# Attention output stored once in fp32 and split where it is used, and a tenth unit of seven products in the first expert block

## The chip, the cores and the metric

The kernel runs on one core of a Trainium2 chip. A core has a matrix engine (TensorE, PE in the profile), three engines that work on tiles (VectorE, DVE; ScalarE, ACT; GpSimd, POOL) and a sync engine (SyncE, SP) that here only issues DMAs. The metric is the device time of one execution in microseconds; lower is better.

## The reference

An attention with a memory gate writes x, and a gated expert layer works on x:

```python
scores = scale * np.matmul(q, k.transpose(0, 1, 3, 2))     # q, k, v: 4 x 8 heads x 576 x 64
scores = np.where(causal, -1000000000.0, scores)
a = np.exp(scores - scores.max(-1, keepdims=True))
a /= a.sum(-1, keepdims=True) + 1e-09
local = np.matmul(a, v)
mem_out = (phi(q) @ M_prev) / (phi(q) . z_prev + 1e-06)    # phi(x) = elu(x) + 1
x = g * mem_out + (1 - g) * local                          # 2304 tokens x 512
gate, val = x @ w_gate, x @ w_val                          # 512 x 1536 each
out = (silu(gate) * val) @ w_out                           # 1536 x 512
```

All inputs and the output are fp32.

## The kernel before

**Attention.** The 32 heads are 16 pairs. The loop runs over n = 0 to 16; iteration n makes the scores of pair n and the values of pair n-1. The score tiles are `s` in PSUM, `ps`, `pl` and `p` (short, long and last key ranges) in SBUF. The DVE reads scores with a mask and a running maximum, ScalarE takes the exponential, the DVE makes the inverse sums `rs`, and POOL scales `ps`, `pl` and `p` by them; PE transposes the scaled tiles (`tr`, copied to `g`) and multiplies with the values. POOL also splits q and k of the pair after, `qh`, `kh` by a rounding copy and `ql`, `kl` by a subtract, so that a product of fp32 numbers is made of three matmuls, high x high, high x low and low x high. `ph` is phi(q) on the DVE.

**Leaving.** At the end of a pair `leave` takes its 576 columns of x out of PSUM in two parts (256 and 320): ScalarE copies the high part into `xh`, the DVE subtracts it from the PSUM tile into `xl`. Both go to DRAM, into `xdh` and `xdl`.

**Weights.** 12 slices of `w_gate`, `w_val` and `w_out` come as pairs of words (`wraw`); a slice is made of thirds, each taken through a clamp, a move and a word (`third_clamp`, `third_move`, `third_word`: `wa`, `we` and `wr`), split into high and low (`wgh`, `wgl`, `woh`, `wol`) and, made ready, stored to `wdr` and `wdo`. Some thirds are made in the attention loop, one step at the end of an iteration (`EARLY`), most in the first block of the experts.

**Experts.** 36 units, three blocks of 768 tokens (`ORDER`) by 12 slices of 128 of d_ff. Of a block, x stands as four pieces in halves of tokens (i) and of channels (j): `p1` (0,0), `p2` (0,1), `p7` (1,0), `p4` (1,1), each as a high and a low tile. The first `PLAIN` units of the first block use `eight`: four groups of 12 matmuls of 384 columns. All others use `seven`: seven products of 6 matmuls on seven mixtures of the pieces, `p1`, `p2`, `p6`, `p7`, `p5`, `p4`, `p3` in this order, with weight mixtures (`operands`) that the DVE and ScalarE make in the unit before. `p6`, `p5`, `p3` and the second `p7` are mixtures of the pieces (`sums` makes them in `xr`, `xt`, `xm`; `spreads` splits them into high and low). Each unit ends in `weigh`, which multiplies silu of the gate half (`zg`, `zh`) by the value half and splits the result into `uh` (ScalarE) and `ul` (DVE, in `halves`, a step later). The groups of the second matrix, `lower`, three matmuls of 512 columns, run one unit later, a group between two steps.

PE's steps write in turns to two PSUM banks (`ring`), so a step starts when the engines have emptied the bank of the step but one before it.

**What sets the order.** Every engine but SP runs in the order of the code (`queued`, which adds a dependence to every instruction; nearly all instructions therefore stand at its line, L84, in the profile). SP's order is set by a scheduler. In a unit, `plan[k]` lists the work that stands behind step k, and `arrive` what goes into the next unit's plan.

## Time and profile before

| | |
|---|---|
| runs | 612.06 us median of 3 (612.0 to 612.1) |
| profiled execution | 611.38 us, of which the span is 609.6 |
| granted TensorE clock | 0.996 of full speed |
| PE busy | 599.6 us (98%) |
| DVE busy | 485.0 us (80%) |
| ACT busy | 395.2 us (65%) |
| POOL busy | 214.8 us (35%) |
| attention loop | to 187.7 us |
| expert units | from 187.8 us |

The span is the time in which the engines of the profiled execution worked. The median is of other executions; times inside the kernel are from the profiled one. Busy shares are averages over two stages that use the engines differently: POOL, for one, works in the attention loop and in the first expert block, and not after it.

### The profile page before, as it was taken

How to read it: one execution, taken by the hardware profiler on the slowest of the kernel's cores; microseconds unless marked ns; L12 is line 12 of the kernel's file. 1: busy time of each engine (PE TensorE's matmuls, PEld its weight loads, DVE VectorE, ACT ScalarE, POOL GpSimd, SP SyncE). 2: the span in 40 equal slices, each digit the busy share in tenths (PEclk: the TensorE clock that was granted, in tenths of full speed). 3: DMA queues.
4: the chain of work that ended last, by engine and by line, in shares of the span. 5: the costliest groups of instructions: out<-in, count | busy, mean ns of one | idle time of the engine just before them, and what ended most of it. 6: DMA issues, size and time to landing. Idle time of an engine off the chain costs nothing.

```text
span 609.6 us, 11282 instructions
## 1 busy us (share of the span) xinstructions
PE 599.6 (98%) x3794; PEld 531.5 (87%) x3794; DVE 485.0 (80%) x1208; ACT 395.2 (65%) x917; POOL 214.8 (35%) x261
## 2 busy tenths in 40 slices
PE   6999999999999999999999999999999999999997
PEld 4878878778788999999899999999999999999996
DVE  6899999999988998898998665665888765665653
ACT  8788888888876777777656654454456654454442
POOL 7999999999963334334320000000000000000000
PEclk9999999999999999999999999999999999999999
DMA  8456756657337657799556622323755622332212
GB/s 250 133 159 178 255 171 204 215 179 216 141 117 277 187 182 239 239 361 282 192 175 208 217 92 70 112 96 115 232 184 177 211 100 69 107 103 69 70 35 103
DMA packets 49321, 102.46 MB, mean 168 GB/s; under 512 B 7024, under 2 KB 17136, under 8 KB 49264
## 3 DMA queue, kind: packets, MB, share of 16 engines
q1 hardware_dynamic: 48832, 101.32, 51.1%
q8 instruction: 30, 0.49, 0.3%
q10 hardware_dynamic: 432, 0.43, 0.2%
q14 instruction: 27, 0.22, 0.1%
HBM read 74.99 MB, written 26.74 MB: 167 GB/s over the span
## 4 chain that ended last, share of the span: by engine, by line
PE 96%; POOL 1%; DMA 1%; issue 0%; DVE 0%; ACT 0%; SPq 0%; ACTq 0%; DVEq 0%
PE s L84 60%; PE tr L84 36%; DMA qr<-in_qt_dram 1%; POOL ps L84 0%; POOL kl L84 0%; SPq L269 0%; ACT g L84 0%; POOL qh L84 0%; DVE rs L84 0%; ACT wa L84 0%; POOL pl L84 0%; DVE mem L84 0%; DVE pl L84 0%; SPq L560 0%; DVE pt L84 0%
## 5 line engine op out<-in xcount | busy, mean ns | idle before, releaser
L84 ACT ACTIVATE zh<-zh 128x384 f32<-128x384 f32 x33 | 17.4, 527 | 74.8 <-DVE zh L84 74.8
L84 POOL TENSOR_SCALAR pl<-pl,rs,og 128x384 f32<-128x384 f32 (+1 forms) x64 | 55.9, 886 | 9.4 <-DVE rs L84 9.4
L84 DVE TENSOR_TENSOR zv<-s,zv 128x384 f32<-128x384 f32 x33 | 18.4, 557 | 51.1 <-PE s L84 45.9
L84 PE MATMUL tr<-woh,ul 128*128 128x512 f32 x144 | 57.3, 398 | 0.0
L84 PE MATMUL tr<-woh,uh 128*128 128x512 f32 x144 | 57.0, 396 | 0.0
L84 PE MATMUL tr<-wol,uh 128*128 128x512 f32 x144 | 56.8, 394 | 0.0
L84 POOL TENSOR_SCALAR we<-we 128x512 f32<-128x512 f32 x32 | 24.9, 780 | 76.8 <-ACT we L84 76.7
L84 ACT ACTIVATE pl<-pl,mx 128x384 f32<-128x384 f32 (+1 forms) x64 | 42.3, 664 | 12.3 <-DVE mx L84 12.3
L84 PE MATMUL tr<-g,vp 128*64 128x320 f32 (+4 forms) x448 | 48.8, 360 | 0.3 <-ACT g L84 0.3
L84 DVE TENSOR_TENSOR tl<-tt,th 128x512 fp32r<-128x512 f32 x66 | 47.7, 723 | 0.0
L84 ACT CAST th<-tt 128x512 fp32r<-128x512 f32 x66 | 41.1, 622 | 9.6 <-DVE tt L84 6.3
L84 PEld LDWEIGHTS tr<-g,vp 128*64 128x64 f32 x448 | 29.4, 137 | 18.0 <-issue 2.3
L84 PE MATMUL s<-kh,qh 64*128 64x128 f32 (+4 forms) x160 | 37.2, 386 | 4.5 <-ACT kh L84 4.0
L84 ACT CAST uh<-zh 128x384 fp32r<-128x384 f32 x36 | 18.5, 513 | 32.6 <-DVE zh L84 32.3
L84 DVE TENSOR_TENSOR zg<-s,zp 128x384 f32<-128x384 f32 x33 | 18.4, 558 | 25.8 <-ACT bh L84 23.5
L84 DVE CUSTOM_DVE_ANT_0 pl<-s,maskp 128x384 f32<-128x384 f32 (+1 forms) x64 | 38.1, 615 | 0.3 <-PE s L84 0.3
L84 DVE TENSOR_TENSOR bl<-wr,bh 128x512 fp32r<-128x512 f32 x66 | 36.3, 550 | 0.0
L84 ACT CAST bh<-wr 128x512 fp32r<-128x512 f32 x66 | 33.9, 513 | 0.0
L84 PEld LDWEIGHTS tr<-woh,ul 128*128 128x128 f32 x144 | 27.1, 188 | 6.8 <-DVE ul L84 0.3
L84 ACT ACTIVATE ps<-ps,mx 128x128 f32<-128x128 f32 (+1 forms) x64 | 28.6, 453 | 6.4 <-DVE mx L84 6.4
L84 POOL TENSOR_SCALAR ps<-ps,rs,og 128x128 f32<-128x128 f32 (+1 forms) x64 | 32.0, 513 | 1.6 <-DVE rs L84 1.2
L84 DVE COPY g<-tr 128x384 f32<-128x384 f32 (+2 forms) x60 | 30.0, 518 | 2.7 <-PE tr L84 1.4
(198 smaller groups left out, 2000.4 us busy)
## 6 DMA issues: line engine op xcount, KB each, us to landing
wr<-wdr SPq DMA_DIRECT2D x24, 512.0 KB, 3.3
wraw<-in_wg_dram SPq DMA_DIRECT2D x12, 512.0 KB, 4.6
wraw<-in_wv_dram SPq DMA_DIRECT2D x12, 512.0 KB, 5.1
wraw<-in_wo_dram SPq DMA_DIRECT2D x12, 512.0 KB, 5.1
wol<-wdo SPq DMA_DIRECT2D x24, 256.0 KB, 2.8
woh<-wdo SPq DMA_DIRECT2D x24, 256.0 KB, 3.1
qr<-in_qt_dram SPq DMA_DIRECT2D x15, 384.0 KB, 3.2
vp<-in_v_dram SPq DMA_DIRECT2D x16, 320.0 KB, 4.1
```

What stands on the lines that cost most here:

```text
L84: ins = getattr(eng, name)(*args, **kw)
```

## The change

x is stored once, as fp32 (`xo` to `xd`), and split into high and low where it is used.

- `leave`: ScalarE copies both parts from PSUM into `xo`; the DVE has no part in it. One store in place of two.
- The first block's four pieces are loaded into their low tiles at the end of iterations 6, 8, 10 and 12. Behind it ScalarE rounds a half (384 columns) of a piece into its high tile per iteration (7 to 14), and an iteration later (8 to 15) the DVE subtracts it in place.
- `PLAIN` is 2: unit 2 is a seven-product unit, and its operands are made a unit earlier, in unit 1.
- `sums` loads the four pieces from `xd` (`begin`) and doesn't add anything; in the first block too, where the sums were taken from the high and low tiles in SBUF. The mixtures `xt`, `xm` and those written into `xr` are as before.
- At a block's end `p1`, `p2` and `p4` are split on chip too, as `p7` was; before, their high and low tiles were loaded.
- In `seven`, of the two `weigh` operations behind the last product, the one that reads its bank goes first, except in the last unit.
- `lower` runs in the order 0 to 5 in all units; before, in 3, 4, 5, 0, 1, 2 from unit 4 on.

```diff
@@ -29,7 +29,7 @@
-PLAIN = 3
+PLAIN = 2
@@ -52,8 +52,7 @@
     dram = ctx.enter_context(tc.tile_pool(name="dram", bufs=1, space=DRAM))
-    xdh = dram.tile([128, NPAIR, NT], F32, name="xdh")
-    xdl = dram.tile([128, NPAIR, NT], F32, name="xdl")
+    xd = dram.tile([128, NPAIR, NT], F32, name="xd")
@@ -165,9 +164,14 @@
 
     xs = {p: [near.tile([128, 2, N2], F32R, name=f"x{p}{part}") for part in "hl"] for p in ("p1", "p2", "p7", "p4")}
 
+    where = dict(p1=(0, 0), p2=(0, 1), p7=(1, 0), p4=(1, 1))
+
+    def x_block(t0, i, j):
+        return xd[:, 2 * j : 2 * j + 2, t0 + i * N2 : t0 + i * N2 + N2]
+
     thirds = [(0, 0), (0, 1), (0, 2), (1, 0), (1, 1)]
-    work_of = [[(3, 0), (3, 1)]]
+    work_of = [[(2, 0), (2, 1)]]
     work_of += [[(n, 2)] + [(n + 1 + (n >= PLAIN - 1), j) for j in range(2)] for n in range(1, NF - 2)]
@@ -505,11 +509,6 @@
-            def give(self, t0, src):
-                c = slice(t0 * 128, t0 * 128 + src.shape[1])
-                act.copy(self.xh[:, c], src)
-                return lambda: dve.tensor_tensor(self.xl[:, c], src, self.xh[:, c].bitcast(F32), op=ALU.subtract)
-
             def turns(self):
                 self.g1 = rot(sb, "g1", [128, 2, 384], F32, 1)
                 self.g2 = rot(sb, "g2", [128, 4, 2, 320], F32, 1)
@@ -540,19 +539,14 @@
 
             def leave(self):
                 first, rest = self.av
-                self.xh = rot(sb, "xh", [128, 576], F32R, NX)
-                self.xl = rot(sb, "xl", [128, 576], F32R, NX)
-                self.give(0, first[:, 0:256])()
+                x = rot(sb, "xo", [128, 576], F32, NX)
+                act.copy(x[:, 0:256], first[:, 0:256])
 
                 def ending():
-                    low = self.give(2, rest[:, 0:320])
-                    return lambda: (low(), self.d2())
+                    act.copy(x[:, 256:576], rest[:, 0:320])
+                    SP.dma_start(xd[:, self.pr, self.b * S : self.b * S + S], x)
 
                 return ending
-
-            def d2(self):
-                for dst, src in ((xdh, self.xh), (xdl, self.xl)):
-                    SP.dma_start(dst[:, self.pr, self.b * S : self.b * S + S], src.bitcast(F32))
...
@@ -576,13 +570,12 @@
                 cur.begin()
             if old:
                 old.turns()
-            low = ending()
+            ending()
             while copies:
                 copies.pop(0)()
             reads = [scores(t) for t in range(2)]
             reads[0](0)
             reads[0](1)
-            low()
             if n == 0:
                 cur.lows()
             reads[1](0)
@@ -680,10 +673,19 @@
                     third_word(act, dve, i, copies)
                 if n == at + 4 and i < 3:
                     low_part(dve)
+            for p, at in zip(("p1", "p2", "p7", "p4"), (6, 8, 10, 12)):
+                high, low = xs[p]
+                if n == at:
+                    SP.dma_start(low.bitcast(F32), x_block(ORDER[0], *where[p]))
+                for k in range(2):
+                    if n == at + 1 + k:
+                        act.copy(high[:, k], low[:, k].bitcast(F32))
+                    if n == at + 2 + k:
+                        dve.tensor_tensor(low[:, k], low[:, k].bitcast(F32), high[:, k].bitcast(F32), op=ALU.subtract)
             if n in AHEAD:
                 raw_load(AHEAD.index(n), loads.get(n + 2))
 
-        ending()()
+        ending()
         low_part(dve)
         i = len(EARLY) + 1
         third_clamp(pool, i)
@@ -739,42 +741,22 @@
         for p in ("p6", "p5", "p3"):
             xs[p] = [mbp.tile([128, 2, N2], F32R, name=f"x{p}{part}") for part in "hl"]
 
-        def block(x, t0, i, j):
-            return x[:, 2 * j : 2 * j + 2, t0 + i * N2 : t0 + i * N2 + N2]
-
-        def direct(t0, p, i, j):
-            for dst, src in zip(xs[p], (xdh, xdl)):
-                SP.dma_start(dst.bitcast(F32), block(src, t0, i, j))
-
-        def sums(t0, here=False):
+        def sums(t0):
 
             got = rot(mbp, "xr", [128, 4, 2, N2], F32, 1)
-            at = ((1, 0), (1, 1), (0, 0), (0, 1))
             a21, a22, a11, a12 = (got[:, n] for n in range(4))
             s1, s = (rot(mbp, name, [128, 2, N2], F32, 1) for name in ("xt", "xm"))
-            tmp = (s, s1)
-            mix = dict(p6=s, p7=a11, p5=s1, p3=a12)
-
-            def load(n):
-                for dst, src in ((got[:, n], xdh), (tmp[n % 2], xdl)):
-                    ld = SP.dma_start(dst, block(src, t0, *at[n]))
-                    follow(ld, last[DVE], "the loads that come before go first", mybir.DependencyClass.Sync)
-
-            def add(n):
-                if here:
-                    h, l = (x.bitcast(F32) for x in xs[("p7", "p4", "p1", "p2")[n]])
-                    dve.tensor_tensor(got[:, n], h, l, op=ALU.add)
-                    return
-                dve.tensor_tensor(got[:, n], got[:, n], tmp[n % 2], op=ALU.add)
-                if n + 2 < 4:
-                    load(n + 2)
+            mix = dict(p1=a11, p2=a12, p6=s, p7=a11, p5=s1, p4=a22, p3=a12)
+
+            def begin():
+                for n, at in enumerate(((1, 0), (1, 1), (0, 0), (0, 1))):
+                    SP.dma_start(got[:, n], x_block(t0, *at))
 
             tt = lambda out, a, b, op: (lambda: dve.tensor_tensor(out, a, b, op=op))
-            work = [lambda n=n: add(n) for n in range(4)] + [
-                tt(s1, a21, a22, ALU.add), tt(s, s1, a11, ALU.subtract), tt(a12, a12, s, ALU.subtract),
-                tt(a11, a11, a21, ALU.subtract),
-            ]
-            return lambda: (load(0), load(1)), work, mix
+            return begin, [
+                tt(s1, a21, a22, ALU.add), tt(s, s1, a11, ALU.subtract),
+                tt(a11, a11, a21, ALU.subtract), tt(a12, a12, s, ALU.subtract),
+            ], mix
 
         def high(mix, p, k):
             return lambda: act.copy(xs[p][0][:, k], mix[p][:, k])
@@ -907,14 +889,13 @@
             dve.tensor_tensor(g2, step(5, "p4", False), g2, op=ALU.add)
             act.activation(g2, g2, AF.Silu, scale=W_ONE)
             rest(5)
-            weigh(u, 1, g2, v2)
-            weigh(u, 0, g1, step(6, "p3", False))
+            ps = step(6, "p3", False)
+            for i, g, v in ((1, g2, v2), (0, g1, ps)) if final else ((0, g1, ps), (1, g2, v2)):
+                weigh(u, i, g, v)
             rest(6)
             return u
 
         first = units[0][0]
-        for p, i, j in (("p1", 0, 0), ("p2", 0, 1), ("p7", 1, 0), ("p4", 1, 1)):
-            direct(first, p, i, j)
         before = None
         spreads = lambda mix, *what: [
             (high if kind == "h" else low)(mix, p, k) for kind, p in what for k in range(2)
@@ -946,56 +927,44 @@
             arrive = []
             if plain:
                 if f == 0:
-                    _, due, mix = sums(t0, True)
-                    for k, some_ in enumerate(((0,), (1,), (2, 4), (3,))):
-                        plan[k] += [due[i] for i in some_]
+                    begin, due, mix = sums(t0)
+                    begin()
+                    plan[1].append(due[0])
+                    plan[2].append(due[1])
+                    plan[3].append(due[2])
                 if f == 1:
-                    for k in range(3):
-                        plan[k].append(due[5 + k])
-                    for k, p in ((0, "p5"), (2, "p6")):
-                        plan[k] += spreads(mix, ("h", p))
-                        plan[k + 1] += spreads(mix, ("l", p))
-                if f == PLAIN - 1:
-                    plan[0] += spreads(mix, ("h", "p3"))
-                    plan[2] += spreads(mix, ("l", "p3"))
-                    arrive = [(0, spreads(mix, ("h", "p7"))), (1, spreads(mix, ("l", "p7")))]
+                    plan[0] += spreads(mix, ("h", "p6"))
+                    plan[1] += spreads(mix, ("l", "p6"))
+                    plan[2] += [due[3]] + spreads(mix, ("h", "p5"))
+                    arrive = [
+                        (0, spreads(mix, ("l", "p5"), ("h", "p7"))), (1, spreads(mix, ("l", "p7"))),
+                        (2, spreads(mix, ("h", "p3"))), (3, spreads(mix, ("l", "p3"))),
+                    ]
             if not end:
                 follows = ORDER[ORDER.index(t0) + 1]
-                if t0 == first and left in (5, 4, 3):
-                    if left == 5:
-                        begin, due, mix = sums(follows)
-                        begin()
-                    plan[5].append(due[5 - left])
-                if not plain:
-                    if left == 3 and t0 != first:
-                        begin, due, mix = sums(follows)
-                        plan[3].append(begin)
-                    if left == 2:
-                        for k, work in zip((5,), due[3:]) if t0 == first else zip((2, 4, 6), due):
-                            plan[k].append(work)
-                    if left == 1:
-                        for k, work in zip((1, 3, 5), due[4:]) if t0 == first else zip((1, 2, 4, 6), due[3:]):
-                            plan[k].append(work)
-                    if left == 0:
-                        plan[2].append(due[7])
-                        plan[3] += spreads(mix, ("h", "p6"))
-                        plan[4] += spreads(mix, ("l", "p6"), ("h", "p7"))
-                        plan[6] += spreads(mix, ("l", "p7"))
-                        arrive = [
-                            (1, spreads(mix, ("h", "p5"))), (2, spreads(mix, ("l", "p5"))),
-                            (3, spreads(mix, ("h", "p3"))), (4, spreads(mix, ("l", "p3"))),
-                        ]
+                if left == 3:
+                    begin, due, mix = sums(follows)
+                    plan[3].append(begin)
+                if left == 1:
+                    plan[2].append(due[0])
+                    plan[5].append(due[1])
+                if left == 0:
+                    plan[1] += spreads(mix, ("h", "p1"))
+                    plan[2] += spreads(mix, ("l", "p1"), ("h", "p2"))
+                    plan[3] += [due[2]] + spreads(mix, ("l", "p2"), ("h", "p6"))
+                    plan[4] += spreads(mix, ("l", "p6"), ("h", "p7")) + [due[3]]
+                    plan[6] += spreads(mix, ("l", "p7"))
+                    arrive = [
+                        (0, spreads(mix, ("h", "p5"))), (1, spreads(mix, ("l", "p5"), ("h", "p4"))),
+                        (2, spreads(mix, ("l", "p4"), ("h", "p3"))), (3, spreads(mix, ("l", "p3"))),
+                    ]
             down = [] if before is None else [
-                lambda j=j, before=before: lower(*before, j) for j in (range(2 * nj) if n <= PLAIN else TURN)
+                lambda j=j, before=before: lower(*before, j) for j in range(2 * nj)
             ]
             if plain:
                 before = (unit, eight(f, down, plan))
             else:
-                before = (unit, seven(ready.pop(n), down, plan, (0, 2, 4) if f else (3, 5, 6)))
-            if not end and left == 0:
-                direct(follows, "p1", 0, 0)
-                direct(follows, "p2", 0, 1)
-                direct(follows, "p4", 1, 1)
+                before = (unit, seven(ready.pop(n), down, plan, (0, 2, 4) if f else (3, 5, 6), n == len(units) - 1))
         halves()
         for j in TURN:
             lower(*before, j)
```

Three places in the engines' instruction order. The DVE in an attention iteration, around the step of a weight third, before (`xl` is the low part of x, `wa` the third, `ps` the next pair's scores; a number behind a name is that of its buffer):

```order
L84 RECIPROCAL rs_244<-rs_244 128x4
L84 SCALAR_TENSOR_TENSOR ph_240<-qe_241,ph_240 128x640
L84 TENSOR_TENSOR rs_279<-sm_152,tiny 128x1
L84 RECIPROCAL rs_279<-rs_279 128x1
L84 TENSOR_TENSOR xl_567<-tr_298,xh_566 128x256
L84 TENSOR_SCALAR wa_1453<-wraw_1015 128x512
L84 ISA ps_271,mx_255<-s_161,maskp 128x128
L84 ISA mx_255 128x1
L84 ISA ps_273,mx_255<-s_162,maskp 128x128
L84 ISA mx_255 128x1
L84 TENSOR_TENSOR xl_567<-tr_303,xh_566 128x320
```

and in the change:

```order
L83 RECIPROCAL rs_243<-rs_243 128x4
L83 SCALAR_TENSOR_TENSOR ph_239<-qe_240,ph_239 128x640
L83 TENSOR_TENSOR rs_278<-sm_151,tiny 128x1
L83 RECIPROCAL rs_278<-rs_278 128x1
L83 TENSOR_SCALAR wa_1430<-wraw_999 128x512
L83 TENSOR_TENSOR xp1l<-xp1l,xp1h 128x384
L83 ISA ps_270,mx_254<-s_160,maskp 128x128
L83 ISA mx_254 128x1
L83 ISA ps_272,mx_254<-s_161,maskp 128x128
L83 ISA mx_254 128x1
```

The two `xl` subtracts from PSUM (`tr`) are gone, and a subtract between SBUF tiles stands behind the third. This is the first of eight.

SP's queue at the end of attention, before:

```order
L555 DMA xdh<-xh_566 128x576
L555 DMA xdl<-xl_567 128x576
L185 DMA wraw_1015<-in_wv_dram 128x1024
L232 DMA wdr<-wr_2563 128x512
L185 DMA wraw_1600<-in_wo_dram 128x1024
L232 DMA wdr<-wr_2563 128x512
L185 DMA wraw_1895<-in_wg_dram 128x1024
```

and in the change:

```order
L547 DMA xd<-xo_561 128x576
L189 DMA wraw_999<-in_wv_dram 128x1024
L236 DMA wdr<-wr_2532 128x512
L753 DMA xr_2548<-xd 128x2x384 x4
L189 DMA wraw_1579<-in_wo_dram 128x1024
L236 DMA wdr<-wr_2532 128x512
```

One store of x is gone, and four loads of pieces of x stand between the store of `wr` and the next load of weights.

The DVE in the first expert unit and at the start of the second (`zg`, `zh` with `s` are `weigh`, `ul` the low part of its result, `wr` a word of a weight), before:

```order
L84 SCALAR_TENSOR_TENSOR wr_2563<-we_1747,wr_2563 128x512
L84 TENSOR_TENSOR xr_2587<-xp7h,xp7l 128x768
L84 SCALAR_TENSOR_TENSOR zg_2602<-s_153,zg_2602 128x384
L84 SCALAR_TENSOR_TENSOR wr_2563<-we_573,wr_2563 128x512
L84 TENSOR_TENSOR xr_2587<-xp4h,xp4l 128x768
L84 TENSOR_TENSOR ul_2625<-zg_2602,uh_2624 128x384
L84 TENSOR_TENSOR xr_2587<-xp1h,xp1l 128x768
L84 TENSOR_TENSOR xt_2588<-xr_2587 128x768
L84 SCALAR_TENSOR_TENSOR zh_2647<-s_153,zh_2647 128x384
L84 TENSOR_TENSOR xr_2587<-xp2h,xp2l 128x768
```

and in the change:

```order
L83 SCALAR_TENSOR_TENSOR wr_2532<-we_1723,wr_2532 128x512
L83 SCALAR_TENSOR_TENSOR zg_2567<-s_152,zg_2567 128x384
L83 SCALAR_TENSOR_TENSOR wr_2532<-we_566,wr_2532 128x512
L83 TENSOR_TENSOR xt_2549<-xr_2548 128x768
L83 TENSOR_TENSOR ul_2589<-zg_2567,uh_2588 128x384
L83 TENSOR_TENSOR xm_2550<-xt_2549,xr_2548 128x768
L83 SCALAR_TENSOR_TENSOR zh_2611<-s_152,zh_2611 128x384
L83 TENSOR_TENSOR xr_2548<-xr_2548 128x768
L83 TENSOR_TENSOR ul_2628<-zh_2611,uh_2627 128x384
```

The adds of high and low into `xr` are gone; `xt` and `xm`, the mixtures of loaded pieces, stand ahead of the `weigh` of `zh`.

## Rows read from the trace of the kernel before

**Rows 1.** Timeline of POOL: start us, us, operation, idle before it and its releaser

```profile
13.82 2.83 POOL L84 TENSOR_SCALAR pl<-pl,rs,og 128x384 f32<-128x384 f32 x4
...
100.18 1.45 POOL L84 TENSOR_TENSOR kl<-kr,kh 128x576 fp32r<-128x576 f32 x1
102.04 3.46 POOL L84 TENSOR_SCALAR pl<-pl,rs,og 128x384 f32<-128x384 f32 x4 [0.41 <-DVE rs L84]
...
112.90 3.73 POOL L84 TENSOR_SCALAR pl<-pl,rs,og 128x384 f32<-128x384 f32 x4 [0.41 <-DVE rs L84]
...
124.05 3.73 POOL L84 TENSOR_SCALAR pl<-pl,rs,og 128x384 f32<-128x384 f32 x4 [0.41 <-DVE rs L84]
...
168.11 3.73 POOL L84 TENSOR_SCALAR pl<-pl,rs,og 128x384 f32<-128x384 f32 x4 [0.41 <-DVE rs L84]
...
178.85 2.82 POOL L84 TENSOR_SCALAR pl<-pl,rs,og 128x384 f32<-128x384 f32 x4 [3.48 <-DVE rs L84]
```

**Rows 2.** Timeline of the DVE in attention, beside the `pl` groups

```profile
101.29 0.36 DVE L84 TENSOR_TENSOR rs<-sm,tiny 128x4 f32<-128x4 f32 x1
...
102.76 0.42 DVE L84 TENSOR_TENSOR xl<-tr,xh 128x256 fp32r<-128x256 f32 x1
103.10 0.44 DVE L84 TENSOR_SCALAR wa<-wraw 128x512 int32<-128x512 int32 x1
...
113.96 0.70 DVE L84 SCALAR_TENSOR_TENSOR wa<-we,wa 128x512 int32<-128x512 int32 x1
...
180.27 0.49 DVE L84 TENSOR_TENSOR xl<-tr,xh 128x320 fp32r<-128x320 f32 x1 [0.21 <-ACT xh L84]
```

**Rows 3.** Timeline of POOL, single operations of three `pl` groups

```profile
103.10 0.90 POOL L84 TENSOR_SCALAR pl<-pl,rs,og 128x384 f32<-128x384 f32 x1
...
113.96 1.16 POOL L84 TENSOR_SCALAR pl<-pl,rs,og 128x384 f32<-128x384 f32 x1
...
178.85 0.67 POOL L84 TENSOR_SCALAR pl<-pl,rs,og 128x384 f32<-128x384 f32 x1 [3.48 <-DVE rs L84]
```

**Rows 4.** Chain of waits in the experts: start us, us, engine and matmuls

```profile
187.80 16.17 PE s L84 x90
...
267.29 2.33 PE s L84 x12
...
314.20 2.23 PE s L84 x12
...
325.83 2.08 PE s L84 x12
...
328.61 1.04 PE s L84 x6
```

**Rows 5.** Timeline of the DVE in the experts

```profile
197.23 0.54 DVE L84 SCALAR_TENSOR_TENSOR zh<-s,zh 128x384 f32<-128x384 f32 x1
...
301.55 0.94 DVE L84 TENSOR_TENSOR xr<-xr,xt 128x768 f32<-128x768 f32 x1
302.42 0.55 DVE L84 SCALAR_TENSOR_TENSOR zh<-zv,zh 128x384 f32<-128x384 f32 x1
302.89 0.54 DVE L84 SCALAR_TENSOR_TENSOR zg<-s,zg 128x384 f32<-128x384 f32 x1
```

**Rows 6.** Timeline of ScalarE at the end of the last pair but one

```profile
179.81 0.43 ACT L84 CAST xh<-tr 128x320 fp32r<-128x320 f32 x1 [0.45 <-PE tr L84]
```

**Rows 7.** SP's timeline, then the same DMA with KB and us to landing

```profile
191.05 0.32 SPq L232 DMA_DIRECT2D wdr<-wr  x1
...
wdr<-wr SPq DMA_DIRECT2D x1, 256.0 KB, 4.7
```

**Rows 8.** Busy time by stretch: two expert units at the start, one ahead of block two

```profile
187.70:196.15 8.45, 8.45 (x52) 8.42 (x49) 7.63 (x11) 4.94 (x9) 4.44 (x4) 1.00 0.97 351
196.15:208.70 12.55, 12.55 (x69) 11.75 (x68) 12.52 (x19) 7.82 (x16) 3.92 (x4) 1.00 0.67 214
...
314.35:325.83 11.48, 11.48 (x61) 10.46 (x60) 10.88 (x22) 7.96 (x17) 0.00 (x0) 1.00 0.86 296
```

The columns are the stretch (us), its length, busy us and instructions of PE, of PE's weight loads, of DVE, ACT and POOL, the granted clock, the share of the DMA engines in use and GB/s.

More of the change, by code (lines that the diff above doesn't have):

```diff
@@ L565, in attention_moe @@
         nothing = lambda *args: None
-        ending = lambda: nothing
+        ending = nothing
         copies = []
@@ L665, in attention_moe @@
                     cur.weighed(((4, 0),))
-            ending = old.leave() if old else lambda: nothing
+            ending = old.leave() if old else nothing
             if n + 2 < NP:
@@ L877, in eight, with seven @@
             return u
-        def seven(w, down, plan, away_at):
+        def seven(w, down, plan, away_at, final):
             def step(n, p, start, before=None):
```

## The prediction

> **What bounds the kernel now.** The page calls PE busy nearly all the span, but the ends of its matmuls are modelled, so this alone doesn't say that PE sets the pace everywhere. I therefore read each stage by the engine on which nothing is idle.
>
> In the attention loop that engine is POOL. In its timeline [rows 1] an iteration begins with a group of four `pl` and ends with `kl`; `p`, `kh`, `qh`, `ps` and `ql` stand between without a break, and the one gap is the 0.41 us, "<-DVE rs", ahead of the next `pl`. The gap has this size in every iteration from 102.04 to 168.11. It is the DVE's `rs<-sm,tiny` and the reciprocal behind it, and that `rs` is not late by its own work: it starts at 101.29, takes 0.36 us [rows 2] for four columns, and ends at 101.65, just when POOL's `kl` ends (100.18 + 1.45). So the period is POOL's work plus 0.41.
>
> A second look confirms it. The group `pl` takes 3.46 us in one iteration and 3.73 in others, and the next `pl` starts 10.86 us later after the short one (102.04 to 112.90), 11.15 after the long one (112.90 to 124.05) [rows 1]: 0.27 more work on POOL, 0.29 more time. What makes `pl` long stands in single instructions [rows 3]. A `pl` of 384 columns takes 0.67 us where it is free, 0.90 at 103.10, where the DVE runs the clamp of a weight third, and 1.16 at 113.96, where it runs a word (512 columns, both inputs in SBUF); the DVE's operations start at the same instants [rows 2]. The two `xl` subtracts, whose first input is in PSUM, lengthen nothing: in the first iteration the DVE has no work beside the group, and it takes 2.83; in the last both `xl` run beside it (the second at 180.27), and it takes 2.82 [rows 1, 2].
>
> The last period (168.11 to 178.85, 10.74 us) is not POOL's: there POOL sat idle 3.48 us [rows 1]. The MoE is PE's: the chain of waits runs through PE's groups without a break, 12 matmuls in 2.08 us, 6 in 1.04, except that from 267.29 to 314.20 five first steps of a unit take 2.33 (four) or 2.23 (the last) [rows 4].
>
> **The change, part by part.**
>
> *A tenth unit of seven products.* Unit 2 has 42 matmuls of 384 columns where it had 48. Six cost 1.04 us [rows 4]: -1.04.
>
> *The stretched first steps.* The DVE's add into `xr` (0.94 us at 301.55) stands directly ahead of the two `weigh` operations, 302.42 and 302.89 [rows 5], and PE's next step waits for the bank that the second frees. The adds are gone, and the operation that frees the bank now goes first: 4 x 0.25 + 0.15 = -1.15. If PE waited for something else there, 0.
>
> *Attention, what goes.* The DVE loses two `xl` per pair. By the start of the next row the first takes 0.34 us (102.76 to 103.10) [rows 2], the second by its width some 0.40, and the loop is not the DVE's. The clamp or the word that followed the first `xl` starts at 103.10, when POOL's first `pl` ends, so an earlier DVE waits for POOL there. I take 0. Bounds: nothing, or what PE could give if the DVE paced the loop (the faster rival below).
>
> *Attention, what comes.* Eight subtracts `xp?l<-xp?l,xp?h` of 128x384, both inputs in SBUF, one each behind the third's operation in the `pl` windows from 102.04 to 178.85. The nearest row is a 384-column operation of two SBUF inputs in the MoE: `zh<-zv,zh` at 302.42, the next start at 302.89, 0.47 us [rows 5]. From clamp to word the DVE's operation grew by 0.26 (0.44 to 0.70) [rows 2] and the `pl` beside it by 0.26 (0.90 to 1.16) [rows 3], so in this place a microsecond of such DVE work is a microsecond of POOL. So each window's `pl` grows by 0.47. Six of the eight lie ahead of a period that is POOL's (102.04 to 156.95): 6 x 0.47 = +2.82. The one at 168.11 is ahead of the 10.74 period, the one at 178.85 in a stretch in which ScalarE's table load is waited for: 0 each. Bounds: 6 x 0.33 = 2.0, if as much hides here as the clamp hides (0.37 of DVE time, 0.44 less the overlap of 0.07 with the next row, for 0.23 of `pl`: 0.14); 7 x 0.55 = 3.9, by the whole duration of the row and with the seventh.
>
> The Trainium skill says why the two kinds differ (SBUF — State Buffer, section "SBUF: two separate sides"): VectorE and GpSimd share one pair of SBUF ports, which is held exclusively for a whole instruction, by a VectorE operation with two SBUF inputs against a GpSimd one that reads SBUF; PSUM reads don't take it. The trace agrees, with 1.16 against 0.67. With the clock of VectorE: DVE Perf Modes (0.96 GHz, one fp32 element a cycle for two tensors) a subtract would hold the port 384/0.96 = 0.40 us, and the term would be an estimated 2.4, the sum 615.7 instead of 616.1; I keep the row's.
>
> *ScalarE's eight casts* sit in ScalarE's idle time ahead of the second copy of each pair, 0.45 us in the last iteration [rows 6]; ScalarE takes no part in POOL's row. Cost 0; without that cover it would be about 0.4 us in each of eight iterations.
>
> *The first block's sums at the start of the MoE.* Before, the four adds read `xp` tiles in SBUF. Now four pieces of 384 KB come by DMA, on SP behind `wdr<-wr` (191.05 [rows 7]). The DMA engines are full there (share 0.97, 351 GB/s [rows 8]). That `wdr` took 4.7 us to land [rows 7], 195.75; one 288 KB store ahead of it is gone (288 KB at 351 GB/s, -0.84); each piece takes 393 kB / 351 GB/s = 1.12. So the pieces land at about 196.0, 197.1, 198.3 and 199.4. The DVE does in order `xt` (needs two), `ul`, `xm` (needs the third) and then the `weigh` of `zh`, whose bank PE wants for the second group of unit 1, at 187.80 + 5 x 2.09 = 198.25 [rows 4]. Before, that `weigh` ran from 197.23 to 197.77 [rows 5]. Now 198.3 + 0.1 + 0.94 + 0.54 = 199.9: +1.7 of PE waiting. Bounds: 0.5, if the pieces share the engines with the 512 KB load ahead of them and land 1.2 early; 2.8, if they share with the next such load, issued right behind them, and land 1.1 late. Behind that `weigh` stand only DVE operations whose users come a unit later.
>
> *Units 2 and 3* get their operands a unit earlier, while the DVE is busy 12.52 of 12.55 us in unit 1 [rows 8]. It loses four adds of 0.87 (301.55 to 302.42 [rows 5]; 3.5 us), but the lag of 1.7 stands ahead of it: +0.4, bounds 0 and 1.0.
>
> *The block boundaries.* In the last unit of a block the DVE now makes the low parts of `p1` and `p2` as well, and both are read in the next unit's first steps: eight subtracts of 0.47 and two mixes of 0.87, 5.5 us, against four and one, 2.75. At the first boundary the DVE was busy 10.88 of 11.48 us [rows 8]. 2.75 more is some 2.1 over. What PE needs first, the sum into `zh` ahead of the next unit, is then about 0.75 late, and the first `lower` about 0.4: +1.15, bounds 0.2 and 2.1. At the second, with no weight thirds left to make, +0.15 (0 to 0.5).
>
> **Sum.** -1.04 - 1.15 + 2.82 + 1.7 + 0.4 + 1.15 + 0.15 = +4.0. The profiled execution took 611.38 us, 0.68 below the median of the runs, 612.06: it becomes 615.4, and the median 616.1.
>
> **Rivals.**
> 1. *The DVE paces the attention loop.* For it: in the long periods the DVE's operation is 0.26 longer too. Then the removed subtracts are worth up to 0.74 a pair, as far as PE follows. The one period that isn't POOL's, 10.74 [rows 1], is the floor that I take for PE: the six from 102.04 to 168.11 are 66.07, 1.6 over six times it; the eight before them, at the same 0.27 each, have 2.2 more to give. Of these 3.8 the new subtract takes back at most 0.47 - 0.40 = 0.07 where it stands for the second `xl`, 0.4 in six. -3.4, with the other terms (+1.2), gives 609.9; from a gain of 2.4 in the loop on it is faster. Against it: POOL has no gap but the 0.41 in these iterations.
> 2. *POOL is lengthened, but the MoE's new waits are covered*: the pieces land in time and the boundary's work fits. -2.2 + 2.8 gives 612.7, no change that can be told.
> 3. *The subtracts find POOL waiting anyway*, in the shadow of the first `pl`, as long as `xl` left the DVE's place free: attention 0, MoE as above, +1.2: 613.3. Against it: the third's operation stands ahead of the subtract and starts as POOL's first `pl` ends.
> 4. *PE never waits for the bank in the stretched steps* and the change's removal there does nothing: +5.2, 617.3.
>
> **How the numbers follow.** A difference under 0.2% (1.2 us) can't be told from none. My forecast, POOL longer and most of the MoE's waits as above (614 to 618), has 0.62; rival 1 0.14, most of it from a gain of 2.4 on; rival 2 0.10; rival 3 0.08; rival 4 0.06. Slower is the forecast, rival 4 and half of rival 3: 0.72. Faster is most of rival 1, 0.11, same the rest, 0.17. The range leaves out the lower part of rival 1 and the sums of all upper bounds: 611.3 to 618.3.
>
> **What would show it.** In the profile after: `pl` groups of 3.9 and 4.2 us where they took 3.46 and 3.73, from the tenth pair on, with periods of 11.3 and 11.6; the early ones unchanged. PE's pieces of 2.08 in place of 2.33, a PE wait of some 1.7 near 201, in unit 1, and one of about 1 at the first boundary. I am wrong if the periods with an `xp` subtract stay at 10.9 and 11.15, or if the early ones fall below 10.86.

## The result, and the profile after

The changed kernel takes 618.35 us (median of 6 runs, 616.67 to 619.64), the kernel before 612.03 (6 runs, 611.23 to 612.21): a ratio of 1.0106, 95% interval 1.0087 to 1.0124. It is slower, as forecast, by 6.3 us where 4.0 were forecast, and 0.05 above the end of the range. The profiled execution took 618.82 us, its span is 617.0, 7.4 more than before. The expert units start at 191.22 in place of 187.73 (+3.5), and take 425.8 from there to the end of the span in place of 421.9 (+3.9).

POOL's timeline after, `pl` groups of four (start us, us, idle before it), answers to [rows 1]:

```profile
47.82 3.39 POOL L83 TENSOR_SCALAR pl<-pl,rs,og 128x384 f32<-128x384 f32 x4 [0.51 <-DVE rs L83]
...
51.98 0.68 POOL L83 TENSOR_SCALAR kh<-kr 128x576 fp32r<-128x576 f32 x1
52.62 0.73 POOL L83 TENSOR_SCALAR qh<-qr 128x640 fp32r<-128x640 f32 x1
53.74 1.97 POOL L83 TENSOR_SCALAR ps<-ps,rs,og 128x128 f32<-128x128 f32 x4 [0.40 <-ACT ph L83]
...
59.12 3.39 POOL L83 TENSOR_SCALAR pl<-pl,rs,og 128x384 f32<-128x384 f32 x4 [0.48 <-DVE rs L83]
...
92.57 3.39 POOL L83 TENSOR_SCALAR pl<-pl,rs,og 128x384 f32<-128x384 f32 x4 [0.41 <-DVE rs L83]
103.39 3.77 POOL L83 TENSOR_SCALAR pl<-pl,rs,og 128x384 f32<-128x384 f32 x4 [0.41 <-DVE rs L83]
114.56 4.04 POOL L83 TENSOR_SCALAR pl<-pl,rs,og 128x384 f32<-128x384 f32 x4 [0.41 <-DVE rs L83]
...
171.36 4.04 POOL L83 TENSOR_SCALAR pl<-pl,rs,og 128x384 f32<-128x384 f32 x4 [0.41 <-DVE rs L83]
```

From 103.39 on, where the new subtracts stand, the groups are 0.31 longer than in [rows 1] (3.77 for 3.46, 4.04 for 3.73); the six periods from there to 171.36 take 67.97 us, before 66.07: +1.90, and the seventh +0.26. Ahead of it, where only the `xl` subtracts are gone, a group is 0.07 shorter (3.39). Yet the period from 47.82 to 59.12 is 11.30 long, before 10.91 in its place, and POOL has a second gap, 0.40 ahead of `ps`. The DVE's timeline in that iteration says why:

```profile
52.69 0.67 DVE L83 TENSOR_TENSOR rs<-sm,tiny 128x4 f32<-128x4 f32 x1
```

This `rs`, the one for `ps`, comes 0.07 after POOL has begun `qh` (52.62) and ends when `qh` ends (53.35). POOL and the DVE in the same iteration of the kernel before:

```profile
47.06 3.46 POOL L84 TENSOR_SCALAR pl<-pl,rs,og 128x384 f32<-128x384 f32 x4 [0.52 <-DVE rs L84]
...
51.30 0.67 POOL L84 TENSOR_SCALAR kh<-kr 128x576 fp32r<-128x576 f32 x1
51.94 0.73 POOL L84 TENSOR_SCALAR qh<-qr 128x640 fp32r<-128x640 f32 x1
```

```profile
51.92 0.10 DVE L84 TENSOR_TENSOR rs<-sm,tiny 128x4 f32<-128x4 f32 x1
```

There `rs` starts 4.86 after `pl` and `qh` 4.88 after it, so `rs` gets in at `kh`'s end; in the later iterations it comes during `kh` and takes 0.13 to 0.39. In the changed kernel `rs` starts 4.87 after `pl`, as before, but `qh` 4.80 after it, as the group is 0.07 shorter. `rs` has missed `kh`'s end by 0.07 us and waits a whole operation of POOL; the rest of the iteration follows 0.4 later. The same happens in the next iteration (period 11.32, before 10.87).

The margin before was 0.02 us, and earlier iterations of the kernel before miss too, such as that of 11.17 us, whose `rs` takes 0.75 at 40.53. In a run below that has the attention of the kernel before (the order of `weigh` alone), the profiled execution misses by 0.01 in the iteration shown here (period 11.37). Without `xl` every profiled kernel with the add of 1e-9 misses in both.

In the experts, PE's, the DVE's and the DMA's part in unit 1 (PE's timeline, the DVE's timeline, the chain of waits) answers to [rows 4, 5, 7]:

```profile
204.19 0.45 PE L83 MATMUL s<-xp1h,wgh 128*128 128x384 f32 x1 [2.29 <-DVE zh L83]
```

```profile
201.37 0.96 DVE L83 TENSOR_TENSOR xt<-xr 128x768 f32<-128x768 f32 x1 [4.11 <-issue]
202.25 0.55 DVE L83 TENSOR_TENSOR ul<-zg,uh 128x384 fp32r<-128x384 f32 x1
202.72 0.95 DVE L83 TENSOR_TENSOR xm<-xt,xr 128x768 f32<-128x768 f32 x1
203.58 0.55 DVE L83 SCALAR_TENSOR_TENSOR zh<-s,zh 128x384 f32<-128x384 f32 x1
```

```profile
193.24 0.61 SPq L236
...
193.95 6.29 DMA xr<-xd
200.24 1.14 issue
201.37 0.96 DVE xt L83
```

The chain runs, as the prediction has it, from the store of `wr` on SP through the loads, `xt`, `xm` and the `weigh` of `zh` to PE. The DVE stands idle 4.11 us for the loads, the first of which takes 6.29 us to land; the four land in turn, 6.3, 6.9, 7.1 and 7.4 us after their issue, 1.0 to 1.1 us apart. The store of `wr` ahead of them (DMA issues, KB and us to landing):

```profile
wdr<-wr SPq DMA_DIRECT2D x1, 256.0 KB, 6.0
```

It is issued at 193.24 and so lands 8.0 us after the start of the experts, as it did before (191.05 and 4.7 us, [rows 7], with a start at 187.73). PE's other waits that weren't there before:

```profile
223.98 0.45 PE L83 MATMUL s<-xp4h,th 128*128 128x384 f32 x1 [0.83 <-ACT zv L83]
...
331.94 0.45 PE L83 MATMUL s<-xp1h,bh 128*128 128x384 f32 x1 [0.60 <-DVE zh L83]
```

By the starts of PE's matmuls (what lies between two, less 0.17 or 0.23 for one), PE loses 2.57 us in unit 1, 1.37 in unit 2, 1.56 at the first block boundary and 0.56 at the second. The 1.1 us of the stretched steps [rows 4] are gone: the first steps of units 7 to 11 run without a gap.

### The profile page after: what moved, and what is told of

Same layout as the page of the kernel before. It is cut to its first block, busy times and chain, and to the rows that moved or that the text cites. A ratio compares the mean times of both kernels' runs of the same rounds, so it can differ in the third digit from the quotient of the medians.

```text
span 617.0 us, 11193 instructions
## 1 busy us (share of the span) xinstructions
PE 601.6 (97%) x3788; PEld 530.6 (86%) x3788; DVE 475.0 (77%) x1192; ACT 403.4 (65%) x942; POOL 217.0 (35%) x261
## 4 chain that ended last, share of the span: by engine, by line
PE 85%; DVE 7%; ACT 3%; DMA 2%; issue 1%; SPq 0%; POOL 0%; DVEq 0%; ACTq 0%
PE s L83 52%; PE tr L83 34%; DMA xr<-xd 1%; DMA kr<-in_kt_dram 1%; DVE xr L83 1%; DVE tt L83 1%; DVE tl L83 1%; DVE zg L83 0%; DVE xp7l L83 0%; DVE zh L83 0%; DVE xp6l L83 0%; ACT pl L83 0%; DVE ul L83 0%; ACT g L83 0%; DVE rs L83 0%
## 5 line engine op out<-in xcount | busy, mean ns | idle before, releaser
L83 POOL TENSOR_SCALAR pl<-pl,rs,og 128x384 f32<-128x384 f32 (+1 forms) x64 | 58.0, 920 | 9.9 <-DVE rs L83 9.9
L83 ACT CAST uh<-zg 128x384 fp32r<-128x384 f32 x36 | 18.5, 514 | 38.0 <-DVE zg L83 37.9
L83 DVE TENSOR_TENSOR bl<-wr,bh 128x512 fp32r<-128x512 f32 x68 | 37.8, 556 | 0.0
L83 DVE TENSOR_TENSOR zh<-s,zh 128x384 f32<-128x384 f32 x34 | 18.9, 556 | 18.7 <-PE s L83 18.7
```

Of the source, the lines that this page charges most:

```text
L83: ins = getattr(eng, name)(*args, **kw)
```

## The experiments

In each, the kernel before ran on the same chip.

**One subtract more, from SBUF and from PSUM.** Both are the kernel before with this line at the end of iterations 1 to 14, `junk` being a tile of its own:

```diff
+            if 1 <= n <= 14:
+                dve.tensor_tensor(junk, old.xl[:, 0:256], old.xh[:, 0:256], op=ALU.subtract)      # or, in the second,
+                dve.tensor_tensor(junk, old.av[0][:, 0:256], old.xh[:, 0:256], op=ALU.subtract)
```

> The kernel before, with one subtract more on VectorE at the end of each iteration 1 to 14, behind the weight third: 128x256, both inputs in SBUF (the xl and xh of the pair before), into a tile that nothing reads. Theory 1 (VectorE operations with two SBUF inputs hold up GpSimd, which paces the attention loop): each costs about 0.25 to 0.34 us of a pl group and of the period, 13 periods, +3 to +4.4 us. Theory 2 (VectorE's own time paces the loop): the same +4.4. The two differ in the next run. Theory 3 (the loop has slack): 0.

> The same as the run before it, in the same place and width, but with the first input in PSUM (the values that the subtract of the first xl reads). Theory 1: a PSUM input leaves GpSimd alone, the pl groups keep 3.46 and 3.73 us, 0 to +1 us in all. Theory 2: as the run before, +4.4 us.

The first takes 615.08 us (ratio 1.0042, 1.0028 to 1.0056), the second 617.27 (1.0078, 1.0061 to 1.0095). The one that should have cost nothing costs more. POOL's rows show theory 1 right on the groups and neither theory right on the period. With the SBUF input, then with the PSUM input:

```profile
104.54 3.70 POOL L84 TENSOR_SCALAR pl<-pl,rs,og 128x384 f32<-128x384 f32 x4 [0.41 <-DVE rs L84]
```

```profile
104.33 3.45 POOL L84 TENSOR_SCALAR pl<-pl,rs,og 128x384 f32<-128x384 f32 x4 [0.50 <-DVE rs L84]
107.77 0.81 POOL L84 TENSOR_SCALAR p<-p,rs,og 128x576 f32<-128x576 f32 x1
108.56 0.67 POOL L84 TENSOR_SCALAR kh<-kr 128x576 fp32r<-128x576 f32 x1
109.20 0.73 POOL L84 TENSOR_SCALAR qh<-qr 128x640 fp32r<-128x640 f32 x1
110.33 1.96 POOL L84 TENSOR_SCALAR ps<-ps,rs,og 128x128 f32<-128x128 f32 x4 [0.40 <-ACT ph L84]
```

The SBUF subtract lengthens `pl` by 0.24 and the period by 0.24 (11.10 and 11.38). The PSUM subtract leaves `pl` at 3.45, as theory 1 says, but the period is 11.39. The DVE comes 5.07 us after the start of `pl` to the next `rs`, in the kernel before 4.65 (106.69 and 102.04), as its timelines show, first with the SBUF, then with the PSUM input:

```profile
109.60 0.10 DVE L84 TENSOR_TENSOR rs<-sm,tiny 128x4 f32<-128x4 f32 x1
```

```profile
109.40 0.54 DVE L84 TENSOR_TENSOR rs<-sm,tiny 128x4 f32<-128x4 f32 x1
```

With the SBUF input the DVE is as late (5.06), but POOL is later too, by 0.24, and `rs` comes as `kh` ends (109.01 + 0.68). With the PSUM input POOL is on time, `qh` runs since 109.20, and `rs` waits for its end. That is the same missed end as in the changed kernel's early iterations.

**The subtracts from PSUM alone taken out.** The kernel before without `xl`, the high part being stored in its place:

```diff
-                return lambda: dve.tensor_tensor(self.xl[:, c], src, self.xh[:, c].bitcast(F32), op=ALU.subtract)
+                return lambda: None
```

> The kernel before without the two xl subtracts per pair; the high part is stored in place of the low one, which is left out of the computation. Theory 1: nothing gained, and if the early iterations of the changed kernel are slower because VectorE, rid of xl, meets GpSimd's operations at another moment, 0 to +1.4 us with periods of 11.3 in the first iterations. Theory 2 (VectorE paces the loop): -2 to -3.5 us.

612.35 us, 1.0003 (0.9993 to 1.0012). VectorE's 0.74 us per pair buys nothing. Four periods of 11.29 to 11.32 have the second gap, two of them where the changed kernel has them, and most others are 0.1 shorter. From the first `pl` to the last the profiled execution is 0.94 longer than that of the kernel before (165.98 for 165.03); the medians show no difference.

**The split of the first block's pieces taken out, or moved.** Twice the changed kernel: once without casts and subtracts, once with the subtracts at the end of iteration 15, in 16 and behind it:

```diff
-                        act.copy(high[:, k], low[:, k].bitcast(F32))
-                        dve.tensor_tensor(low[:, k], low[:, k].bitcast(F32), high[:, k].bitcast(F32), op=ALU.subtract)
+                    SP.dma_start(high.bitcast(F32), x_block(ORDER[0], *where[p]))
...
+                lows_of("p1")      # n == 15; "p2" in 16, "p7" and "p4" behind the loop
```

> The changed kernel without the split of the first block's four pieces: high and low tiles are both loaded with x as it is, and ScalarE's eight casts and VectorE's eight subtracts are left out. Theory 1: the pl groups from the ninth iteration on return to 3.4 and 3.65 us, and seven periods lose 0.31 each: 2.2 us below the changed kernel, 616.2. What is left of the attention's +3.5 us, 1.35, then has another cause, the subtracts from PSUM that are gone. Rival (ScalarE's casts or the loads cost it): the pl groups shorten but the time stays above 617.5.

> The changed kernel with the eight subtracts moved out of the seven iterations that GpSimd paces: p1's two stand at the end of iteration 15, p2's in iteration 16, p7's and p4's behind it. The casts stay. If the subtracts cost the loop 0.31 us each by holding up GpSimd, the pl groups return to 3.4 and 3.65 and the first expert unit starts 1.5 to 2.2 us earlier, 616.5. If the loop is slower for another reason (the casts, the loads), the groups shorten and the start stays.

616.86 us (1.0067, 1.0048 to 1.0087) and 618.58 (1.0120, 1.0105 to 1.0136). In both the groups are 3.37 to 3.40 and 3.64 to 3.66 up to the last but one, and from the first `pl` to the last the loop takes 165.8 and 166.0 us in place of 168.0: the subtracts, and not the casts, which the second keeps, cost 2.0 to 2.2. What is left over the 165.0 of the kernel before, 0.8 to 1.0, is there without either subtract. The second run shows no gain in the end. Its experts start 2.1 us earlier, but PE waits 3.05 in unit 1, for the same loads, which in this run are issued 4.0 us after the start of the experts (193.11) in place of 2.7, behind a load of weights that waits for ScalarE; and then PE runs slower for a while. Its stretches (length, busy us of PE, its weight loads, DVE, ACT, POOL, granted clock, DMA share, GB/s):

```profile
199.50:203.00 3.50, 0.45 (x3) 0.16 (x2) 3.06 (x5) 0.18 (x1) 0.00 (x0) 1.00 1.06 401
203.00:207.00 4.00, 4.00 (x14) 3.88 (x15) 2.79 (x5) 2.97 (x6) 0.32 (x1) 0.58 0.85 310
207.00:212.00 5.00, 5.00 (x27) 4.49 (x26) 5.00 (x9) 5.00 (x12) 2.04 (x3) 1.00 0.95 301
```

**The order of `weigh`, the tenth unit, and the first block's sums.** The first two put parts of the change into the kernel before, the last two take parts out of the changed kernel:

```diff
-            weigh(u, 1, g2, v2)      # kernel before; the second run has also
-            weigh(u, 0, g1, step(6, "p3", False))        # PLAIN = 2 and the change's places of mixtures
+            ps = step(6, "p3", False)
+            for i, g, v in ((1, g2, v2), (0, g1, ps)) if final else ((0, g1, ps), (1, g2, v2)):
+                weigh(u, i, g, v)
...
-                    begin()      # third run, the changed kernel
+                h, l = (x.bitcast(F32) for x in xs[("p7", "p4", "p1", "p2")[n]])
+                dve.tensor_tensor(got[:, n], h, l, op=ALU.add)
...
-PLAIN = 2      # fourth run, the changed kernel
+PLAIN = 3
```

> The kernel before with one part of the change, the new order of the two weigh operations (the one that reads the bank goes first, except in the last unit). Theory (PE waits in five first steps for the bank that the second weigh frees): the add into xr stays ahead, but the bank is free 0.47 us earlier, more than the 0.23 of waiting: pieces of 2.33 become 2.08, -1.1 us, 610.9. Rival (the add alone sets the wait): the pieces stay at 2.33, 0.

> The kernel before with two parts of the change, the order of weigh and the tenth unit of seven products (its operands a unit earlier); x is left and stored as before, and the sums of the first block are taken from SBUF. Theory: -1.1 from the order, -1.04 from the unit, and VectorE's margin in units 1 and 2 costs +0.3 to +1.4: 610.2 to 611.3. Rival (VectorE can't carry the operands a unit earlier): PE waits over 2 us in units 1 and 2, 612 or more.

> The changed kernel with the first block's sums added up from the high and low tiles in SBUF again, so that the four loads behind the store of wr are gone and VectorE has its four adds back. Theory (the loads' landing holds the weigh of zh, and with it PE in unit 1, and all that VectorE does behind it): PE's wait of 2.5 us in unit 1 goes, of the 1.4 in unit 2 about half: -3 us, 615.3. Rival (VectorE's work, not the loads, is what is late): with 3.5 us more on VectorE PE waits as long or longer, 618 or more.

> The changed kernel with nine units of seven products in the first block again, the operands and mixtures a unit later. Theory (the tenth unit's earlier operands cost PE 1.4 us in unit 2 and save 1.04): those waits go, +1.04 - 1.4 = -0.4, 618.0, and the wait in unit 1 stays 2.5 us. Rival (the tenth unit saves in full): +1.04, 619.4.

The order alone gives 611.67, 0.9998 (0.9988 to 1.0008). Its chain of waits shows that the wait only moves:

```profile
280.08 2.08 PE s L84 x12
282.16 0.46 PE tr L84 x2
282.63 0.00 issue
282.63 0.50 PE tr L84
```

The twelve matmuls are down to 2.08, but the third one of the `lower` behind them, which reads `ul`, waits. The DVE's timeline shows for which:

```profile
281.56 0.54 DVE L84 TENSOR_TENSOR ul<-zg,uh 128x384 fp32r<-128x384 f32 x1
282.03 0.54 DVE L84 TENSOR_TENSOR ul<-zh,uh 128x384 fp32r<-128x384 f32 x1
```

PE goes on at 282.63, behind the second `ul` (282.57). This run keeps the order 3, 4, 5, 0, 1, 2 of `lower`, whose first three groups read the half that the new order of `weigh` takes second. The `ul` of the other half, which the change's order 0 to 5 reads first, was done at 282.10, before PE got there (282.46, 0.23 after the second matmul of the group). So the run shows that the order of `weigh` alone is worth nothing; whether the gain of the changed kernel in this place comes from the adds that are gone or from the two orders together stays open, as neither was run by itself.

Order and tenth unit in the kernel before: 613.93, 1.0041 (1.0026 to 1.0055). PE loses 1.75 us in the second product of unit 2 and 1.1 in its sixth, more than the 1.04 that the unit saves; the second theory is right, but for the place, as unit 1 has no wait. The changed kernel with sums from SBUF: 616.76, 1.0085 (1.0070 to 1.0100). PE's timelines in unit 2, with order and tenth unit in the kernel before, then with sums from SBUF in the changed one:

```profile
211.16 0.44 PE L84 MATMUL s<-xp2h,bh 128*128 128x384 f32 x1 [1.48 <-DVE zh L84]
```

```profile
214.03 0.45 PE L83 MATMUL s<-xp2h,bh 128*128 128x384 f32 x1 [0.55 <-DVE zh L83]
```

With sums from SBUF the wait of 2.57 in unit 1 is gone, and unit 2 loses 2.0 in place of 1.37 (0.8 of it at this product, where the changed kernel loses 0.24); the experts take 423.9 in place of 425.8. The changed kernel with nine units: 618.60, 1.0111 (1.0096 to 1.0126); PE waits 2.0 in unit 1 in place of 2.57, and 0.6 in its first unit of seven products (now unit 3) in place of 1.37, and the experts take 425.6 in place of 425.8: in the changed kernel the tenth unit is worth nothing that can be told, since VectorE is late with its operands.

**The add of 1e-9 taken out.** In the kernel before, in the changed one, and in the one with the extra PSUM subtract:

```diff
-                    dve.tensor_tensor(rs, self.sm[:, c : c + n], tiny[:, 0:n], op=ALU.add)
+                    dve.reciprocal(rs, self.sm[:, c : c + n])
```

> The kernel before without the add of 1e-9 ahead of the reciprocal of the sums (rs is the reciprocal of sm itself; a sum of exponentials with their maximum taken off is at least 1, and the add leaves it as it is). The add has two inputs in SBUF, the reciprocal one. If VectorE waits there for GpSimd's running operation, the gap of 0.41 us ahead of pl falls to 0.1 or 0.2 and PE's own period of 10.75 is what is left: 10.86 becomes 10.75 and 11.15 about 10.85, -2 to -3 us, 609.5. If the gap is the way of a semaphore and the two operations' own time, the gap falls by 0.13 and the time by 1 us or less.

> The kernel before with the extra subtract from PSUM in each iteration, which cost 5 us though it left the pl groups as they were, and without the add ahead of the reciprocal. If the 5 us came from the add missing the end of GpSimd's operation (rs 0.54 to 0.65 us in place of 0.13 to 0.36), they go: periods of 10.9 to 11.1, within 1 us of the kernel before without the add. If VectorE's 0.33 us more of work itself sets the period, they stay at 11.2 or more.

> The changed kernel without the same add. If the iterations of 11.3 us with short pl groups (four early ones) come from VectorE's add coming just after a start on GpSimd and waiting 0.5 to 0.65 us for its end, they return to under 11, and the gap ahead of pl shrinks everywhere: the first expert unit starts 3 to 4 us earlier, 614.5 to 615.5. If those iterations have another cause, they stay at 11.3.

The kernel before without the add takes 607.51 us, 0.9949 (0.9929 to 0.9969), the fastest median of all here; five of its seven runs lie at 607 to 608 and two at 610.5, for which no profile shows the cause. With the PSUM subtract that cost 5 us it takes 608.23, 0.9949 (0.9934 to 0.9964). POOL's timeline of the first:

```profile
108.58 1.44 POOL L84 TENSOR_TENSOR kl<-kr,kh 128x576 fp32r<-128x576 f32 x1
109.99 3.88 POOL L84 TENSOR_SCALAR pl<-pl,rs,og 128x384 f32<-128x384 f32 x4
```

The 0.41 ahead of `pl` is gone. From the fourth on, periods are 10.55 to 10.86 in place of 10.86 to 11.16, and with the PSUM subtract 10.65 to 10.96 where they were 11.37 to 11.65 (the last, 10.74 and 11.07, left out). So it was the add's wait for POOL, not VectorE's work, that made 5 us of a subtract of 0.33 us per iteration.

The changed kernel, however, takes 621.05, 1.0150 (1.0132 to 1.0168). Its early periods are 10.4 to 10.9, as expected, but two others are 14.7 long. The DVE's timeline in both and POOL's in the first of them:

```profile
120.85 4.03 DVE L83 SCALAR_TENSOR_TENSOR ph<-qe,ph 128x640 f32<-128x640 f32 x1
...
157.43 3.98 DVE L83 SCALAR_TENSOR_TENSOR ph<-qe,ph 128x640 f32<-128x640 f32 x1
```

```profile
119.95 1.45 POOL L83 TENSOR_TENSOR kl<-kr,kh 128x576 fp32r<-128x576 f32 x1
121.37 2.84 POOL L83 TENSOR_SCALAR pl<-pl,rs,og 128x384 f32<-128x384 f32 x4
```

`ph`, two SBUF inputs, came while `kl` ran, and POOL went from `kl` through all four `pl` without letting it in: 4.03 us for an operation of 0.80, with PE waiting behind it (2.67 us at 127.17). With the add, the gap ahead of `pl` let it in. In the kernel before without the add it also comes while `kl` runs, and gets in behind it:

```profile
109.79 0.91 DVE L84 SCALAR_TENSOR_TENSOR ph<-qe,ph 128x640 f32<-128x640 f32 x1
```

What differs in the rows is when it comes. Where `pl` follows `kl`, in both kernels without the add, `ph` got in when it came up to 0.48 us before `kl`'s end; in the two long periods it came 0.56 and 0.51 before it. These are two cases, and why it is so stays open.

## Why the prediction was wrong

The direction and most mechanisms were right; the sum was 4.0 and the measured difference 6.3. In the profiles it is 7.4, which the terms make up as follows: PE's new waits in the experts came out 2.7 above the forecast, what goes from attention 0.8 above it, what comes 0.7 below it, and 0.5 stands ahead of the first `pl`. So two kinds of term failed: the 0 for what goes, whose reason was wrong, and the lateness in the experts, which was put too low in all four places.

- *Attention, what comes*: right in kind. +2.82 was forecast for six windows at 0.47; they cost 0.31 each, 1.90, with 0.26 from the seventh, which I had put at nothing because I took its period of 10.74 for PE's. It is no floor: without the add the loop runs at 10.55 to 10.86. The subtract's price was read from VectorE's row. Against groups without either subtract (3.39 and 3.65) it is 0.38, near the 0.40 of the prediction's second estimate; POOL got back 0.07 from the `xl` that are gone, of which the prediction had read that they lengthen nothing.
- *Attention, what goes*: this step failed. "I take 0" holds for the median of the kernel without `xl`, but not for the reason given. That the loop is POOL's was read as: the DVE's time doesn't matter. It matters through where its two-input operations fall among POOL's. I had seen `rs` waiting for `kl` and asked what a longer POOL does, not what happens to the other `rs`, ahead of `ps`, if POOL comes 0.07 us earlier. It cost 0.82 in the eight periods ahead of the new subtracts in the profiled run: 0.84 in the two that miss `kh`'s end, 0.26 in the first period, and the others 0.28 shorter. Another 0.5 was there from the first `pl` on, and kernels with the same first iterations differ by as much (13.61 to 14.77), so it isn't put down to the change.
- *Stretched steps*: -1.15 forecast, -1.1 measured. The new order of `weigh` alone is worth nothing; whether the adds that are gone were needed, or the order of `lower` would have done, was not run.
- *Tenth unit and units 2 and 3*: the -1.04 is there, but the 0.4 for lateness was 1.37. The forecast put it down to the lag of the loads; with the tenth unit in the kernel before, which has no such loads, unit 2 loses 2.85, so VectorE's work alone makes it late. Together the unit is worth nothing that can be told (425.8 us of experts with it, 425.6 without; medians 618.35 and 618.60). Mis-sized: VectorE's load in unit 1, 12.52 of 12.55 us busy [rows 8], should have been taken as full.
- *First sums*: +1.7 forecast, 2.57 measured, within its bounds. The chain is the one forecast, and the pieces land in turn, 1.0 to 1.1 us apart where 1.12 was forecast. What failed is the 0.84 taken off for the store of x that is gone: the store of `wr` landed 8.0 us after the start of the experts in both kernels, so all that stands behind it was that much later than forecast. VectorE stood idle 4.11 us here, so this wait is the loads' and not its work's; with sums from SBUF it goes, and 0.6 comes back in unit 2.
- *Boundaries*: +1.15 and +0.15 forecast, 1.56 and 0.56 measured. At the first, PE waits 0.88 for `zh` and 0.37 in the first `lower` for `ul`, close to the 0.75 and 0.4 of the forecast, and 0.31 in the last product of the unit before, which was not in it; at the second 0.20 there and 0.36 for `ul`. That VectorE's added work is the cause is read from these rows; no run takes it out.

Rival 1, the DVE pacing the loop, is refuted: without `xl` nothing is gained, and the 5 us that a PSUM subtract costs go with the add of 1e-9. Rival 2 is refuted by PE's waits in the experts, 6.1 us, rival 3 by the groups that are 0.31 longer, rival 4 by the gaps of the stretched steps that are gone. Of the prediction's signs, "the early ones unchanged" did not come, and one early period did fall below 10.86 (10.82, from 92.57 to 103.39); its group is 0.07 shorter and it has no second gap, so that sign didn't tell of the rival that it stood for. The range ended at +6.2 and left out the sum of all upper bounds, +8.1. The time came out above it because all four terms of lateness were too low at once, three of them for VectorE's work and one for the loads; the price of the new subtracts, too high by 0.7, made up for a part of that by luck.

## What to carry to other kernels

Where operations of two engines hold each other up, as GpSimd's and VectorE's with two SBUF inputs do here, a small one is priced by where it falls: it waits for the other engine's whole operation, and a shift of 0.07 us cost 0.4 in an iteration. Look for such operations on the loop's path and make them one-input ones (here an add of 1e-9 to a sum that is at least 1: -4.0 us by the median, though two of seven runs gained only 1.0); but see who loses the gap that the wait had left. Taking work off an engine that the loop doesn't wait for gains nothing, and may move what is left on it to a worse moment.

## What the runs showed of the hardware

- VectorE's operation with two SBUF inputs, 0.80 us by itself, took 4.03, while GpSimd ran the rest of `kl` and four `pl` back to back; its turn came only behind the fifth. In other iterations, where it came nearer to `kl`'s end, it got in behind `kl` (0.91 us at 109.79). By the Trainium skill (SBUF — State Buffer, "SBUF: two separate sides") the second to start blocks until the first has finished. That fits `rs`, which took up to 0.75 us where it met a running operation of GpSimd and 0.10 at the least; for `ph` the measurement goes further, five operations of the other engine in a row.
- After PE's wait of 3.05 us in unit 1 the granted clock was 0.58 over the next 4 us, the matmuls of 384 columns starting 0.32 us apart in place of 0.17, the lower of the two levels (1.2 for 2.4 GHz), some 1.6 us lost. The length of the wait doesn't decide it: the wait of 2.29 in the profile of the changed kernel was followed by a granted clock of 1.00, but one of 2.03 without the split by 0.56 (202.4 to 205.6 us), and one of 1.81 without the add by 0.57 (205 to 209), with the same 0.32 apart.
